# Pooled attention and expert routing on one core: batches in pairs, pooling by accumulated transposes, x scattered straight into expert slots

## The chip, the cores and the metric

One core of a Trainium2 chip. The metric is the device time of one execution in microseconds (us); where several executions are given, the median. The kernel before takes 391.01 us (two runs, 390.69 and 391.33).

A ratio is the mean time of one kernel's fast runs over the mean of the other's fast runs of the same rounds, so it is not quite the ratio of the medians that are quoted. Its interval is at 95%. "Fast" leaves out runs marked slow (a lower clock, or over 1.5% above the fastest of the same kernel).

## The reference

Attention in which keys and values are averaged over groups of 8 positions (576 become 72), then a layer of experts in which each token's expert is given.

```python
B, H, S, D = 8, 8, 576, 64
k_p = k.reshape(B, H, 72, 8, D).mean(axis=3)        # and v_p
scores = (1/8) * q @ k_p.T                          # softmax over 72
x = attn(q, k_p, v_p) -> [B*S = 4608, H*D = 512]
for e in range(8):                                  # domain_id: int64[4608], 0..7
    mask = domain_id == e
    out[mask] = relu(x[mask] @ w1[e]) @ w2[e]       # w1 512x1024, w2 1024x512
```

All inputs are float32, the sums are float32 in the kernel and the operands float16. The draw is fixed: the experts have 497 to 615 tokens.

## The kernel before

Attention runs batch by batch. x is written to memory in token order, then, when the last batch is stored, each expert gathers its rows (6 blocks of 128, 704 columns used), transposes them on TensorE, and runs two layers. The parts that matter:

```python
# attention: divide by the softmax sum, plain order in x_sb
nc.vector.tensor_tensor(out=x_sb[0:rows, g, D*h0:D*(h0+4)]..., in0=xq[0:rows, :, 1:65],
                        in1=rcp[0:rows, :].to_broadcast([rows, 4, D]), op=ALU.mult)
nc.sync.dma_start(dst, x_sb[:, 0:4, :])              # x_nat, once per batch
# ... cut ...
# experts: gather, transpose on PE, two layers, scatter
for j in range(6):
    nc.gpsimd.indirect_dma_start(out=gth[:, j], in_=x_nat[:], in_offset=orig_sb[:, e, j:j+1], ...)
# ... cut ...
osem = nc.alloc_semaphore(f"osem{e}")
with tc.tile_critical(name=f"osc{e}"):
    for j in range(6):
        nc.gpsimd.indirect_dma_start(out=out, out_offset=orig_sb[0:rows, e, j:j+1], 
                                     in_=o_sb[0:rows, j, :], ...).then_inc(osem, 16)
    nc.gpsimd.wait_ge(osem, 16 * 6)                  # one wait for all six
if e + 2 < E:
    gs[e + 2] = moe_xload(e + 2, ...)
    wlds[(e + 2) % 3] = moe_wload_hw(e + 2)          # float32 by the ScalarE queue, cast on VectorE
```

The six output scatters of an expert go out one behind the other and are waited for once, at the end. The weights of experts 2 to 7 do not go through GpSimd's queue at all: they are fetched as float32 on another queue and cast on VectorE.

The softmax here doesn't subtract the row's maximum and nothing guards it: scores larger than these inputs give would overflow.

Of the kernel before, what the change touches and what calls it, by code (L numbers as in the profile page):

```python
# [9 lines left out]
BF16 = mybir.dt.bfloat16  # L10
I32 = mybir.dt.int32
U32 = mybir.dt.uint32

AFT = mybir.ActivationFunctionType
ALU = mybir.AluOpType

B = 8
H = 8
S = 576
D = 64  # L20
HD = H * D
SP = S // 8
N = B * S
FF = 1024
E = 8
CAP = 704
CAPB = 768
NSLOT = E * CAPB
NBLK = NSLOT // 128
SENT = 1 << 20  # L30
NCH = 36
# [3 lines left out]
def kernel(  # L35
# [11 lines left out]

    const = ctx.enter_context(tc.tile_pool(name="const", bufs=1))
    dram = ctx.enter_context(tc.tile_pool(name="dram", bufs=1, space=bass.MemoryType.DRAM))
    persist = ctx.enter_context(tc.tile_pool(name="persist", bufs=1))  # L50

    x_nat = dram.tile([N, HD], F16)

    iota_row = const.tile([128, 128], I32)
    nc.gpsimd.iota(iota_row[:], pattern=[[1, 128]], base=0, channel_multiplier=0)
    iota_col = const.tile([128, 1], I32)
    nc.gpsimd.iota(iota_col[:], pattern=[[0, 1]], base=0, channel_multiplier=1)
    iota_row_f = const.tile([128, 128], F32)
    nc.vector.tensor_copy(iota_row_f[:], iota_row[:])
    iota_col_f = const.tile([128, 1], F32)  # L60
    nc.vector.tensor_copy(iota_col_f[:], iota_col[:])
    ident_f = const.tile([128, 128], F32)
    nc.vector.tensor_scalar(out=ident_f[:], in0=iota_row_f[:], scalar1=iota_col_f[:, 0:1],
                            scalar2=None, op0=ALU.is_equal)
    ident_h = const.tile([128, 128], F16)
    nc.vector.tensor_copy(ident_h[:], ident_f[:])
    Ls = const.tile([128, 128], F32)
    nc.vector.tensor_scalar(out=Ls[:], in0=iota_row_f[:], scalar1=iota_col_f[:, 0:1],
                            scalar2=None, op0=ALU.is_gt)
    ones_row = const.tile([128, 128], F32)  # L70
    nc.vector.memset(ones_row[:], 1.0)
    def band_tile(name, w, off, ncols):
        bt = const.tile([128, ncols], F16, name=name)
        pw = const.tile([128, 1], F32, name=name + "_pw")
        nc.vector.tensor_scalar(out=pw[:], in0=iota_col_f[:], scalar1=1.0 / w, scalar2=float(off),
                                op0=ALU.mult, op1=ALU.add)
        pwm1 = const.tile([128, 1], F32, name=name + "_pwm1")
        nc.vector.tensor_scalar(out=pwm1[:], in0=pw[:], scalar1=-1.0, scalar2=None, op0=ALU.add)
        q1 = const.tile([128, ncols], F32, name=name + "_q1")
        nc.vector.tensor_scalar(out=q1[:], in0=iota_row_f[:, 0:ncols], scalar1=pw[:, 0:1],  # L80
                                scalar2=None, op0=ALU.is_le)
        q2 = const.tile([128, ncols], F32, name=name + "_q2")
        nc.vector.tensor_scalar(out=q2[:], in0=iota_row_f[:, 0:ncols], scalar1=pwm1[:, 0:1],
                                scalar2=None, op0=ALU.is_gt)
        nc.vector.tensor_tensor(q1[:], q1[:], q2[:], op=ALU.mult)
        nc.vector.tensor_scalar(out=bt[:], in0=q1[:], scalar1=0.125, scalar2=None, op0=ALU.mult)
        return bt
    P2 = band_tile("P2", 2, 0, 64)
    Ptail = band_tile("Ptail", 8, 0, 8)
    tokid_i = const.tile([128, NCH], I32)  # L90
    nc.gpsimd.iota(tokid_i[:], pattern=[[1, NCH]], base=1, channel_multiplier=NCH)
    tokhi_i = const.tile([128, NCH], I32)
    nc.vector.tensor_scalar(out=tokhi_i[:], in0=tokid_i[:], scalar1=6, scalar2=None,
                            op0=ALU.logical_shift_right)
    toklo_i = const.tile([128, NCH], I32)
    nc.vector.tensor_scalar(out=toklo_i[:], in0=tokid_i[:], scalar1=63, scalar2=None,
                            op0=ALU.bitwise_and)
    tokhi = const.tile([128, NCH], F32)
    nc.vector.tensor_copy(tokhi[:], tokhi_i[:])
    toklo = const.tile([128, NCH], F32)  # L100
    nc.vector.tensor_copy(toklo[:], toklo_i[:])

    orig_sb = persist.tile([128, E, 6], I32)
    posf = persist.tile([128, NCH], F32)
    blkf = persist.tile([128, NCH], F32)

    def pe_warmup(wps, n_mm, mv, k_parts=128):
        for i in range(n_mm):
            nc.tensor.matmul(wps[0:128, 0:512], ident_h[0:k_parts, :], mv,  # L109
                             start=(i == 0), stop=(i == n_mm - 1))  # L110

    with tc.tile_pool(name="rt", bufs=1) as rt, \
         tc.tile_pool(name="rtp", bufs=1, space=bass.MemoryType.PSUM) as rtp:
        dom2 = rt.tile([128, NCH, 2], I32)
        nc.sync.dma_start(dom2[:], moe_domain_id.bitcast(I32).rearrange(
            "(p c two) -> p c two", p=128, two=2))
        domf = rt.tile([128, NCH], F32)
        nc.vector.tensor_copy(domf[:], dom2[:, :, 0])
        oh = rt.tile([128, NCH, E], F32)
        for e in range(E):  # L120
            nc.vector.tensor_scalar(out=oh[:, :, e], in0=domf[:], scalar1=float(e),
                                    scalar2=None, op0=ALU.is_equal)
        rowtot = rt.tile([128, E], F32)
        nc.vector.tensor_reduce(out=rowtot[:], in_=oh[:].rearrange("p c e -> p e c"),
                                op=ALU.add, axis=mybir.AxisListType.X)
        a_ps = rtp.tile([128, E], F32, space=bass.MemoryType.PSUM)
        nc.tensor.matmul(a_ps[:], Ls[:], rowtot[:], start=True, stop=False)
        erow_i = rt.tile([128, E], I32)
        nc.gpsimd.iota(erow_i[:], pattern=[[1, E]], base=0, channel_multiplier=0)
        erow = rt.tile([128, E], F32)  # L130
        nc.vector.tensor_scalar(out=erow[:], in0=erow_i[:], scalar1=float(CAPB), scalar2=None,
                                op0=ALU.mult)
        nc.tensor.matmul(a_ps[:], ones_row[0:1, :], erow[0:1, :], start=False, stop=True)
        bpre = rt.tile([128, NCH, E], F32)
        nc.vector.memzero(bpre[:, 0, :])
        for c in range(1, NCH):
            nc.vector.tensor_tensor(bpre[:, c, :], bpre[:, c - 1, :], oh[:, c - 1, :], op=ALU.add)
        abase = rt.tile([128, E], F32)
        nc.vector.tensor_copy(abase[:], a_ps[:])
        tmp = rt.tile([128, NCH, E], F32)  # L140
        for e in range(E):
            nc.vector.tensor_scalar(out=tmp[:, :, e], in0=bpre[:, :, e], scalar1=abase[:, e:e + 1],
                                    scalar2=None, op0=ALU.add)
        nc.vector.tensor_tensor(tmp[:].rearrange("p c e -> p (c e)"),
                                tmp[:].rearrange("p c e -> p (c e)"),
                                oh[:].rearrange("p c e -> p (c e)"), op=ALU.mult)
        slotf = rt.tile([128, NCH], F32)
        nc.vector.tensor_reduce(out=slotf[:], in_=tmp[:], op=ALU.add, axis=mybir.AxisListType.X)
        slot_i = rt.tile([128, NCH], I32)
        nc.vector.tensor_copy(slot_i[:], slotf[:])  # L150
        pos_i = rt.tile([128, NCH], I32)
        nc.vector.tensor_scalar(out=pos_i[:], in0=slot_i[:], scalar1=127, scalar2=None,
                                op0=ALU.bitwise_and)
        blk_i = rt.tile([128, NCH], I32)
        nc.vector.tensor_scalar(out=blk_i[:], in0=slot_i[:], scalar1=7, scalar2=None,
                                op0=ALU.logical_shift_right)
        nc.vector.tensor_copy(posf[:], pos_i[:])
        nc.vector.tensor_copy(blkf[:], blk_i[:])
    scale = 1.0 / 8.0
    mw = ctx.enter_context(tc.tile_pool(name="mw", bufs=3))  # L160
    with tc.tile_pool(name="ld", bufs=3) as ld_pool, \
         tc.tile_pool(name="qp", bufs=2) as qp, \
         tc.tile_pool(name="vp_p", bufs=3) as vp_p, \
         tc.tile_pool(name="ap", bufs=3) as ap_pool, \
         tc.tile_pool(name="xp", bufs=2) as xp, \
         tc.tile_pool(name="rt2", bufs=2) as rt2, \
         tc.tile_pool(name="gp_ps", bufs=4, space=bass.MemoryType.PSUM) as gp_ps, \
         tc.tile_pool(name="sct_ps", bufs=1, space=bass.MemoryType.PSUM) as sct_ps, \
         tc.tile_pool(name="op_ps", bufs=1, space=bass.MemoryType.PSUM) as op_pool, \
# [53 lines left out]
        def stage_a(b):  # L223
            k_sb, v_sb, q_sb, k_tl, v_tl, q_tl = ld[b % 3]
            if b + 2 < B:
                ld[(b + 2) % 3] = attn_load(b + 2)
# [271 lines left out]
```

## Time and profile before

| stretch, us | what runs | TensorE (PE) busy |
|---|---|---|
| 0 to 17 | routing | 6 of 17 |
| 17 to 176 | attention, 8 batches of 20 us | 137 of 159 |
| 176 to 195 | hole: x stored, gathered, weights | 7 of 19 |
| 195 to 383 | 8 experts, 23.5 us each | 178 of 188 |
| 383 to 395 | last scatters | 0 |

The table is read from the busy time of each engine by stretch. Columns: stretch and its length, then busy us and instruction count of PE, PE's weight loads, VectorE (DVE), ScalarE (ACT), GpSimd (POOL), then the mean granted PE clock, the DMA share and GB/s. Kernel before:

```profile
0.00:17.00 17.00, 6.17 (x17) 2.73 (x18) 12.55 (x81) 1.72 (x4) 11.95 (x22) 1.00 1.20 142
17.00:57.00 40.00, 33.85 (x291) 20.09 (x289) 32.27 (x104) 21.87 (x36) 18.50 (x24) 0.83 1.56 198
57.00:176.00 119.00, 103.45 (x656) 54.72 (x656) 83.92 (x300) 46.18 (x81) 11.80 (x15) 0.50 0.60 104
176.00:195.00 19.00, 7.46 (x36) 3.42 (x35) 5.05 (x5) 2.15 (x4) 12.62 (x11) 0.59 0.90 336
195.00:383.00 188.00, 178.13 (x1063) 93.37 (x1062) 41.64 (x35) 83.09 (x132) 93.04 (x80) 0.97 0.48 172
```

PE is busy 178 of 188 us in the experts at clock 0.97: that stage is bound by PE, and anything that hides behind PE is free there. In attention the clock is 0.50 for most of the time.

### The profile page before, as it was taken

How to read it: one execution, taken by the hardware profiler on the slowest of the kernel's cores; microseconds unless marked ns; L12 is line 12 of the kernel's file. 1: busy time of each engine (PE TensorE's matmuls, PEld its weight loads, DVE VectorE, ACT ScalarE, POOL GpSimd, SP SyncE). 2: the span in 40 equal slices, each digit the busy share in tenths (PEclk: the TensorE clock that was granted, in tenths of full speed). 3: DMA queues.
4: the chain of work that ended last, by engine and by line, in shares of the span. 5: the costliest groups of instructions: out<-in, count | busy, mean ns of one | idle time of the engine just before them, and what ended most of it. 6: DMA issues, size and time to landing. Idle time of an engine off the chain costs nothing.

```text
span 395.3 us, 5560 instructions
## 1 busy us (share of the span) xinstructions
PE 329.1 (83%) x2060; PEld 174.3 (44%) x2060; DVE 175.4 (44%) x521; ACT 155.1 (39%) x257; POOL 153.7 (39%) x156
## 2 busy tenths in 40 slices
PE   0879879899797979852595999999999999999960
PEld 0445544527272544430252455554545454554420
DVE  6897867676957666692301233322322421001010
ACT  1147716243341616500234345362635355453410
POOL 9445425122000000007875626275266375443405
PEclk9989855555555555555669899999999999999995
DMA  8999999999601010138992729388674523211303
GB/s 108 190 190 192 192 220 196 226 210 195 132 2 60 2 61 0 61 119 313 384 336 63 265 74 337 143 276 322 221 272 129 207 64 124 104 73 52 114 1 128
DMA packets 58027, 62.80 MB, mean 159 GB/s; under 512 B 16140, under 2 KB 43278, under 8 KB 58000
## 3 DMA queue, kind: packets, MB, share of 16 engines
q0 software_dynamic: 46656, 32.53, 45.5%
q10 hardware_dynamic: 9408, 25.17, 17.8%
q1 hardware_dynamic: 1936, 4.76, 3.3%
q8 instruction: 16, 0.26, 0.3%
q14 instruction: 11, 0.09, 0.1%
HBM read 68.19 MB, written 16.25 MB: 214 GB/s over the span
## 4 chain that ended last, share of the span: by engine, by line
PE 45%; DMA 5%; issue 2%; ACT 1%; POOL 1%; DVE 1%; ACTq 0%; POOLq 0%; another core or an unknown queue 0%
PE ops L449 21%; PE hps L438 20%; DMA w_32_2696<-in_moe_w_dram 4%; PE trp L419 3%; POOL out_dram L459 1%; ACT hT L440 1%; DVE w_sb L400 1%; DMA x_nat<-x_sb 0%; ACT xsT_cur L421 0%; DVE o_sb L452 0%; ACT o_sb L454 0%; ACTq L394 0%; POOLq L493 0%; ACTq L398 0%; POOLq L459 0%
## 5 line engine op out<-in xcount | busy, mean ns | idle before, releaser
L408 POOL DMA_INDIRECT gth<-x_nat,orig_sb x48 | 57.0, 1188 | 131.0 <-DVE gth L406 87.4
L449 PE MATMUL ops<-w_sb,hT 128*128 128x512 f16 (+1 forms) x384 | 91.7, 383 | 1.0 <-ACT hT L440 0.7
L438 PE MATMUL hps<-xsT_cur,w_sb 128*128 128x192 f16 (+1 forms) x512 | 83.5, 320 | 2.8 <-ACT hT L440 1.7
L459 POOL DMA_INDIRECT out_dram<-o_sb,orig_sb x48 | 54.4, 1134 | 58.0 <-issue 25.8
L438 PEld LDWEIGHTS <-w_sb 128*128 128x128 f16 x512 | 46.9, 100 | 38.0 <-issue 8.5
L440 ACT ACTIVATE hT<-hps 128x704 f16<-128x704 f32 x64 | 48.4, 756 | 38.8 <-PE hps L438 32.4
L452 DVE COPY o_sb<-ops 128x512 f32<-128x512 f32 x24 | 16.6, 690 | 92.8 <-PE ops L449 84.7
L449 PEld LDWEIGHTS <-hT 128*128 128x128 f16 (+1 forms) x384 | 36.7, 100 | 42.3 <-issue 5.9
L262 PE MATMUL qt_p<-ident_h,q_sb 128*64 128x128 f16 x256 | 35.7, 279 | 5.0 <-ACT qT_sb L266 3.6
L454 ACT ACTIVATE o_sb<-ops 128x512 f32<-128x512 f32 (+1 forms) x24 | 14.3, 595 | 62.6 <-PE ops L449 53.1
L421 ACT ACTIVATE xsT_cur<-trp 128x512 f16<-128x512 f16 (+1 forms) x48 | 24.4, 561 | 30.3 <-DMA gth<-x_nat,orig_sb 24.3
L262 PEld LDWEIGHTS <-q_sb 128*64 128x64 f16 x256 | 24.7, 144 | 17.7 <-issue 15.9
L266 ACT ACTIVATE qT_sb<-qt_p 64x1024 f16<-64x1024 f16 x16 | 16.3, 1018 | 22.7 <-PE qt_p L262 22.7
L317 PEld LDWEIGHTS <-at_sb 72*128 72x128 f16 (+1 forms) x320 | 20.8, 130 | 8.2 <-DVE x_sb L322 3.6
L419 PE MATMUL trp<-ident_h,gth 128*128 128x128 f16 (+1 forms) x192 | 17.2, 222 | 7.6 <-ACT xsT_cur L421 5.5
L419 PEld LDWEIGHTS <-gth 128*128 128x128 f16 (+1 forms) x192 | 13.4, 101 | 17.3 <-issue 13.0
L238 PEld LDWEIGHTS <-P_80 128*64 128x64 f16 x64 | 8.2, 132 | 18.0 <-DVE kp_sb L246 11.5
L297 PEld LDWEIGHTS <-kpT_sb 64*72 64x72 f16 x64 | 9.0, 143 | 16.3 <-issue 14.1
L194 DVE TENSOR_SCALAR ohc<-iota_row_f,posf 128x128 f16<-128x128 f32 x36 | 11.0, 306 | 10.6 <-PE op_ps L204 10.6
L204 PE MATMUL op_ps<-vc,ohc 128*128 128x96 f16 x36 | 7.8, 245 | 8.5 <-DVE vc L202 8.4
L109 PE MATMUL warm_2424<-gth,ident_h 128*128 128x512 f16 x10 | 4.4, 626 | 10.7 <-DMA gth<-x_nat,orig_sb 10.7
L183 POOL DMA_DIRECT2D k_sb<-in_k_dram x8 | 7.1, 888 | 15.8 <-PE op_ps L204 11.4
(621 smaller groups left out, 431.7 us busy)
## 6 DMA issues: line engine op xcount, KB each, us to landing
q_sb<-in_q_dram POOLq DMA_DIRECT2D x8, 512.0 KB
k_sb<-in_k_dram POOLq DMA_DIRECT2D x8, 512.0 KB
v_sb<-in_v_dram POOLq DMA_DIRECT2D x8, 512.0 KB
x_nat<-x_sb SPq DMA_DIRECT2D x8, 512.0 KB, 2.6
w_sb<-in_moe_w_dram POOLq DMA_DIRECT2D x4, 1024.0 KB
w_32_2692<-in_moe_w_dram ACTq DMA_DIRECT2D x1, 2048.0 KB
w_32_2696<-in_moe_w_dram ACTq DMA_DIRECT2D x1, 2048.0 KB
w_32_2919<-in_moe_w_dram ACTq DMA_DIRECT2D x1, 2048.0 KB
```

Source lines behind the costliest of these rows:

```text
L262: nc.tensor.transpose(qt_p[:, hl, t, :], q_sb[:, 2 * hp + hl, t, :], ident_h[:])
L266: nc.scalar.activation(qT_sb[:, 2 * hp:2 * hp + 2, 0:512], qt_p[:], AFT.Copy)
L317: nc.tensor.matmul(xq[0:rows, hh, :], at_sb[0:72, h, cols], vp_sb[0:72, h, :], start=True, stop=True)
L408: nc.gpsimd.indirect_dma_start(out=gth[:, j], out_offset=None, in_=x_nat[:], in_offset=bass.IndirectOffsetOnAxis(ap=orig_sb[:, e, j:j + 1] ...
L419: nc.tensor.transpose(trp[:, kk, 0:cols], gth[0:cols, j, 128 * kk:128 * (kk + 1)], ident_h[0:cols, 0:cols])
L421: nc.scalar.activation(dst[:, :, 128 * j:128 * j + cols], trp[:, :, 0:cols], AFT.Copy)
L438: nc.tensor.matmul(hps[:, c0:c0 + cn], w1_sb[:, kk, 128 * f:128 * (f + 1)], xsT[:, kk, c0:c0 + cn], start=(kk == 0), stop=(kk == 3))
L440: nc.scalar.activation(hT[:, f, :], hps[:, 0:CAP], AFT.Relu)
L449: nc.tensor.matmul(ops[0:rows, :], hT[:, f, 128 * j:128 * j + rows], w2_sb[:, f, :], start=(f == 0), stop=(f == 7))
L452: nc.vector.tensor_copy(o_sb[0:rows, j, :], ops[0:rows, :])
L454: nc.scalar.activation(o_sb[0:rows, j, :], ops[0:rows, :], AFT.Copy)
L459: nc.gpsimd.indirect_dma_start(out=out, out_offset=bass.IndirectOffsetOnAxis(ap=orig_sb[0:rows, e, j:j + 1], axis=0), in_=o_sb[0:rows, j, ...
```

## The change

Its intent: take work off VectorE and PE, and remove the hole and the trip of x through memory in token order. Batches are handled in pairs. Keys and values are loaded in tiles whose partition is a pooling group, so that one load has runs of 18 KB, and PE pools them by transposing the 8 members of each group into the same accumulator. The slot of every token is worked out before attention starts. Each finished block of 128 tokens is scattered directly to its slots in `x_slots` and comes back by DMA transposes, so PE transposes nothing for the experts. An expert has 640 slots, not 704 and 6 blocks; a loop for overflow is there but finds no token. The first 384 slots of experts 0 and 1 may start during the last pair. The core of the diff, cut:

```diff
-            k_sb = ld_pool.tile([128, H, 4, D], F16, tag="k_sb")          # per batch, many short runs
+        t = io.tile([128, 72, D], F16, tag=tag, bufs=2, name=tag)         # per pair, 18 KB runs
+        nc.gpsimd.dma_start(t[:]..., t_ap[2*pr:2*pr+2].rearrange("b h (g t) d -> (b h g) (t d)", g=8))
-                            nc.vector.tensor_reduce(out=dst, in_=src, op=ALU.add, ...)
+                    for t in range(8):                                    # pooled transposes
+                        for half in range(2):
+                            nc.tensor.matmul(pv[64*half:64*half+64, w, :], kk[:, 8*(w0+w)+t, :], ident[:],
+                                             start=(t == 0), stop=(t == 7), skip_group_check=True)
-            nc.sync.dma_start(dst, x_sb[:, 0:4, :])
+            xo = x_sb[:].rearrange("p (b h a) -> p h a b", b=4, h=H)[:, 4 * qd:4 * qd + 4]
+            nc.vector.tensor_tensor(out=xo, in0=pv[:, :, 0:64].rearrange("p h (a b) -> p h a b", b=4), ...)
+            if qd == 1:
+                nc.gpsimd.indirect_dma_start(out=x_slots[:], out_offset=slot_i[:, c:c+1], in_=x_sb[:], ...)
-                    nc.tensor.transpose(trp[:, kk, 0:cols], gth[0:cols, j, 128*kk:128*(kk+1)], ...)
+            nc.sync.dma_start_transpose(xT[:, :, 0:s1 - s0], x_slots[CAP*e + s0:CAP*e + s1, :])
-            w1_32 = ws.tile([128, 4, FF], F32, tag="w1_32")
-            nc.scalar.dma_start(w1_32[:], ...);  nc.vector.tensor_copy(w1_sb[:], w1_32[:])
+            nc.gpsimd.dma_start(w1[:]..., moe_w1[e].rearrange("(p k) f -> p (k f)", k=4))  # all experts
-            with tc.tile_critical(name=f"osc{e}"):                        # six scatters, one wait
+                nc.gpsimd.indirect_dma_start(out=out, out_offset=orig[:, bl:bl+1], in_=y[:], ...)
```

Every GpSimd DMA goes into one software queue (q0 in the trace). Nothing in the diff says that scatters wait for each other, but each one writes `x_slots` or `out` as a whole as far as dependency tracking can see, because the rows are known only at run time. So each one is held back until the previous one has landed. The reordered write of x (`p h a b`) matches the row order of the new `w1` load.

## The prediction

> **What bounds the kernel now.** The engine table by stretch (391.0 us timed, 395.3 profiled) shows four stages. 0 to 17 us: routing. 17 to 176 us: attention, 20 us per batch; until about 100 us the DMA is full (190 to 210 GB/s written, twice that read, as loads cast f32 to f16), afterwards PE and DVE wait on each other; the granted PE clock is 0.50 from 57 to 201 us. 176 to 195 us: a hole, in which x is stored and gathered and a weight load holds the chain 16.3 us (chain of waits). 195 to 383 us: eight experts, PE busy 178 of 195 us at clock 0.96, so PE-bound, 23.5 us each. Tail of scatters: 12 us.
>
> **Removed.** (1) Experts compute 640 columns and 5 blocks instead of 704 and 6. In the trace 64 first-layer matmuls took 9.65 us and 41 second-layer ones 9.07 us, so columns run at 2.4 GHz; 640 slots cost 8.5+8.5=17.1 us per expert, against 9.4+10.2 plus 1.3 of PE transposes and bubbles. All experts: 137 us of PE against a stage of 188. The largest expert has 615 tokens, so the overflow loop should not run. (2) The hole: x goes out as it is made, and two experts' first 384 slots start inside the last pair. (3) DVE's pooling reductions (64 of 0.68 us) and weight casts (12 of 2.3 us). (4) The tail: scatters go out as blocks finish.
>
> **Added.** (1) Routing is longer and stands before attention in PE's order: some 80 DVE instructions (0.17 us small, 0.45 us at 288 elements), 109 small matmuls, four 1152-wide comparisons (estimate 1.3 us) each waiting for PE. Estimate: first pooling matmul at 45 us instead of 16. Loads run meanwhile (six of 2.36 MB, 40 us at the 370 GB/s read rate seen). (2) Pooling on PE: 196 matmuls per pair. With transposes, scores and values, 43k columns per pair: 23 us at full clock, 37 us at half. (3) Each scatter of x and of the output waits until the previous one landed. A 128-row scatter took 2.7 us to land: x costs about 22 us per pair, output 15 us per expert beside PE's 17. (4) Ten DMA transposes, of which this trace has none. The Trainium skill, "DMA: Bandwidth & Descriptors" (other measured facts), gives 261 GB/s: an estimate of 2.5 us plus latency, hidden except after pairs 2 and 3.
>
> **Sum.** Routing 45; first pooling 12; pairs 0 to 2 at 30 each; pair 3 with expert 0's early part 30, including 7 us waiting for pair 2's last scatters; other experts 126 of PE plus 10 of layer turns and 4 waiting; tail 7: about 322 us.
>
> **Clock.** The Trainium skill, "TensorE: Matmul & The Clock Gate" (Part 1), says a busy window releases the half clock and an idle one restores it; the trace agrees in kind (1.00 in most of 17 to 57 us, 0.50 in loosely fed attention, 0.96 with experts). Dense pooling bursts should keep pairs mostly fast; all slow gives about 360, all fast 305.
>
> **What would show it.** Chain: routing until 45 us, then PE. Pair period 27 to 38 us; 17 to 19 us per full expert at clock near 1; DVE busy falls from 175 to about 130 us; POOL's scatters wait on earlier DMAs; PE waits at most about 10 us for xT.
>
> **What would make it wrong.** Transposes far slower than 261 GB/s; serial scatters slowed by weight loads above 3.4 us each, which makes POOL the experts' bound; attention all at half clock; routing longer than 55 us.
>
> Predicted: 322 us, 8 in 10 within 292 to 360; faster by over 2% 0.93, within 2% 0.04, slower 0.03.

## More of the kernel before

The groups of instructions (line, engine, operation, output and input tiles, count, then busy us and mean ns of one, then idle time before the group with what ended it), and one execution of the division that writes x (least, median and most ns, then its start). Kernel before:

```profile
L449 PE MATMUL ops<-w_sb,hT 128*128 128x512 f16 (+1 forms) x384 | 91.7, 383 | 1.0 <-ACT hT L440 0.7
L459 POOL DMA_INDIRECT out_dram<-o_sb,orig_sb x48 | 54.4, 1134 | 58.0 <-issue 25.8
L438 PEld LDWEIGHTS <-w_sb 128*128 128x128 f16 x512 | 46.9, 100 | 38.0 <-issue 8.5
```

```profile
L322 DVE TENSOR_TENSOR x_sb<-b_673,rcp x1: 405/405/405, 46.3 to 46.3; 128x256 f16<-128x256 f32 x1
```

Read the second line for what it does not say: of POOL's 58 us of idle before output scatters, 25.8 us is ended by nothing in the profile ("issue") and the rest by other engines' work, none of it by an earlier DMA. The division takes 0.41 us for 256 columns.

The landing times (from issue until all bytes are written) of the output scatters, least, median and most, first in the kernel before, then in the changed kernel; the third line is that of the changed kernel's x scatters:

```profile
DMA to landing us min/median/max: 2.0/2.7/2.7
DMA to landing us min/median/max: 2.6/2.8/13.1
DMA to landing us min/median/max: 2.4/2.4/26.7
```

## The result and the profile after

Changed kernel: 443.27 us (442.43 and 444.12); before 391.01 us. Ratio 1.1363, interval 1.1241 to 1.1485. The prediction of 322 us, 292 to 360, was wrong in size and direction.

The same stretches for the changed kernel (0 to 47 routing and first pooling, then four pairs, experts, tail):

```profile
0.00:47.00 47.00, 18.33 (x318) 16.55 (x319) 26.70 (x93) 2.79 (x5) 7.16 (x17) 0.75 0.88 191
47.00:80.00 33.00, 25.05 (x380) 19.11 (x378) 27.79 (x45) 16.33 (x26) 5.99 (x6) 0.78 0.38 89
80.00:123.00 43.00, 21.04 (x316) 15.38 (x315) 22.14 (x38) 13.38 (x22) 8.36 (x11) 0.62 0.69 148
123.00:157.00 34.00, 23.06 (x340) 16.87 (x338) 26.11 (x43) 14.59 (x23) 8.98 (x11) 0.70 0.29 71
157.00:223.00 66.00, 28.38 (x204) 16.84 (x204) 28.67 (x47) 14.18 (x23) 14.57 (x16) 0.66 0.30 72
223.00:414.00 191.00, 142.23 (x773) 95.84 (x772) 40.51 (x59) 32.36 (x54) 45.13 (x51) 0.85 0.60 136
414.00:441.00 27.00, 2.06 (x10) 0.73 (x8) 0.69 (x1) 0.60 (x1) 3.92 (x4) 0.61 0.10 38
```

The boundary at 80 us is late: the second pair's first matmul starts at 75.1 us, so the first pair took 28 us and the second 48.

Compare the expert rows. PE's work fell from 178 to 142 us (some of the fall is expert 0's first 384 slots, which ran in the last pair), and the stage still takes 191 us in place of 188: PE is no longer the bound. The last pair needs 66 us for 28 us of PE work.

The groups of instructions of the changed kernel that answer to those of before:

```profile
L514 PEld LDWEIGHTS <-w 128*128 128x128 f16 x512 | 71.9, 149 | 94.1 <-issue 67.0
L442 DVE TENSOR_TENSOR x_sb<-small,rcp 128x256 f16<-128x256 f32 x72 | 93.5, 1299 | 22.9 <-DMA x_slots<-x_sb,slot_i 19.3
L530 PE MATMUL small<-w,hT 128*128 128x512 f16 x320 | 72.8, 386 | 0.3 <-DVE y L535 0.3
L539 POOL DMA_INDIRECT out_dram<-y,orig x40 | 39.8, 995 | 149.1 <-DMA out_dram<-y,orig 117.5
```

The output matmuls (L530) take 386 ns each, as before (383): PE has not become slower. POOL's idle before an output scatter is now ended by an output scatter's own landing, for 117.5 us in all. And the division that writes x takes 1299 ns where it took 405.

The waits of the changed kernel (engine, line, what it waited for: us in all, times, longest):

```profile
POOL out_dram L539 <- DMA out_dram<-y,orig: 117.5, 25, 12.8
...
POOL x_slots L447 <- DMA x_slots<-x_sb,slot_i: 47.1, 9, 26.4
...
PE big L514 <- DMA xT<-x_slots: 42.0, 2, 28.0
```

The timeline of GpSimd (start, duration, instruction, in brackets the idle before it and what ended it) shows one step of each chain. First in the second pair, then in the experts:

```profile
87.76 0.61 POOL L71 DMA_DIRECT2D q<-in_q_dram  x1
88.34 0.59 POOL L486 DMA_DIRECT2D w<-in_moe_w_dram  x1
...
91.70 1.03 POOL L447 DMA_INDIRECT x_slots<-x_sb,slot_i  x1 [1.18 <-DVE x_sb L442]
119.16 1.02 POOL L447 DMA_INDIRECT x_slots<-x_sb,slot_i  x1 [26.42 <-DMA x_slots<-x_sb,slot_i]
```

```profile
262.93 0.60 POOL L486 DMA_DIRECT2D w<-in_moe_w_dram  x1
263.51 0.59 POOL L489 DMA_DIRECT2D w<-in_moe_w_dram  x1
266.12 1.04 POOL L539 DMA_INDIRECT out_dram<-y,orig  x1 [2.03 <-DVE y L535]
279.05 1.01 POOL L539 DMA_INDIRECT out_dram<-y,orig  x1 [11.89 <-DMA out_dram<-y,orig]
```

A scatter of x normally lands in 2.4 us (median). The one issued at 91.70 stands in the same queue behind q, w1, w2, k and v issued from 87.8 on, and lands just before 118.5. Meanwhile no further x block may go out, the buffers of x fill, and PE and DVE stop from about 104 to 119. VectorE's line at the end of that stop:

```profile
118.46 1.30 DVE L442 TENSOR_TENSOR x_sb<-small,rcp 128x256 f16<-128x256 f32 x1 [16.16 <-DMA x_slots<-x_sb,slot_i]
```

In the experts the first scatter after each pair of weight loads lets the next go only 10.7 to 13.9 us later, six times; the others follow at about 3.5 us, or when their block is ready. That sets the length of an expert: its five scatters need about 12 + 4 x 3.5 = 26 us where a load stands between them, against 17.7 us of PE work (8.9 us for the first layer and 8.8 us for the second, read from the last good version below).

The largest stop is in the last pair. PE stands 28 us in the middle of its attention work, because a filled-in piece of expert 0 in its program order waits for the transposed x:

```profile
192.01 1.47 PE L514 MATMUL big<-xT,w 128*128 128x384 f16 x4 [28.00 <-DMA xT<-x_slots]
```

The scatters of the third pair went one by one, and the last landed at about 179 us; then two transposes needed another 12 us beside a weight load. The shortfall by stage, with the terms of the prediction:

| stage | predicted | measured | error |
|---|---|---|---|
| routing | 45 | 37.7 | -7 |
| first pooling | 12 | 9.2 | -3 |
| pairs 0 to 2 | 90 | 110.3 (28, 48, 34) | +20 |
| pair 3 | 30 | 66.2 | +36 |
| experts | 140 | 190.9 | +51 |
| tail | 7 | 26.5 | +19 |
| sum | 324 | 440.8 | +117 |

### The profile page after: what moved, and what is told of

It is laid out like the page before. It is cut to its first block, busy times and chain, and to the rows that moved or that the text cites. A ratio compares the mean times of both kernels' runs of the same rounds, so it can differ in the third digit from the quotient of the medians.

```text
span 440.8 us, 5605 instructions
## 1 busy us (share of the span) xinstructions
PE 260.2 (59%) x2328; PEld 181.3 (41%) x2328; DVE 172.6 (39%) x321; ACT 94.2 (21%) x153; POOL 94.1 (21%) x113
## 5 line engine op out<-in xcount | busy, mean ns | idle before, releaser
L514 PE MATMUL big<-xT,w 128*128 128x320 f16 (+2 forms) x512 | 89.4, 337 | 78.1 <-DMA xT<-x_slots 42.0
L514 PEld LDWEIGHTS <-w 128*128 128x128 f16 x512 | 71.9, 149 | 94.1 <-issue 67.0
L442 DVE TENSOR_TENSOR x_sb<-small,rcp 128x256 f16<-128x256 f32 x72 | 93.5, 1299 | 22.9 <-DMA x_slots<-x_sb,slot_i 19.3
L520 DVE TENSOR_SCALAR hT<-big 128x640 f16<-128x640 f32 (+2 forms) x40 | 28.4, 711 | 122.8 <-PE big L514 120.9
L530 PE MATMUL small<-w,hT 128*128 128x512 f16 x320 | 72.8, 386 | 0.3 <-DVE y L535 0.3
L539 POOL DMA_INDIRECT out_dram<-y,orig x40 | 39.8, 995 | 149.1 <-DMA out_dram<-y,orig 117.5
L447 POOL DMA_INDIRECT x_slots<-x_sb,slot_i x36 | 35.6, 990 | 144.2 <-DVE rcp L439 63.7
L530 PEld LDWEIGHTS <-hT 128*128 128x128 f16 x320 | 31.6, 99 | 36.8 <-issue 2.3
L416 ACT ACTIVATE at<-big 72x576 f16<-72x576 f32 x64 | 40.0, 644 | 27.9 <-PE big L413 26.8
L535 DVE COPY y<-small 128x512 f32<-128x512 f32 x20 | 14.0, 702 | 63.8 <-PE small L530 37.7
L413 PE MATMUL big<-qT,kpT 64*72 64x288 f16 x128 | 24.2, 379 | 10.2 <-DVE hT L520 4.1
## 6 DMA issues: line engine op xcount, KB each, us to landing
x_slots<-zt ACTq DMA_DIRECT2D x1, 1536.0 KB, 19.3
```

The costliest lines, as they stand in the source:

```text
L413: nc.tensor.matmul(p[0:72, par, 0:288], s["kpT"][64 * par:64 * par + 64, bh, :], s["qT"][64 * par:64 * par + 64, :, 8 * bh:8 * bh + 8], st ...
L416: nc.scalar.activation(at[0:72, bh % 8, :].rearrange("p (a c) -> p a c", a=2), p[0:72, :, 0:288], AFT.Exp, scale=1.0 / 64.0)
L442: nc.vector.tensor_tensor(out=xo, in0=pv[:, :, 0:64].rearrange("p h (a b) -> p h a b", b=4), in1=rcp[:].unsqueeze(2).unsqueeze(3).to_broad ...
L447: nc.gpsimd.indirect_dma_start(out=x_slots[:], out_offset=bass.IndirectOffsetOnAxis(ap=slot_i[:, c:c + 1], axis=0), in_=x_sb[:], in_offset ...
L514: nc.tensor.matmul(p[:, a, 0:m], w1[:, kk, fi:FF:8], xT[:, kk, m * a:m * a + m], start=(kk == 0), stop=(kk == 3))
L520: nc.vector.tensor_scalar(out=dst, in0=p[:, 0:nh, 0:m], scalar1=0.0, scalar2=None, op0=ALU.max)
```

## The experiments

Theory A: the time goes to *gates*, scatters that wait for the landing of the previous one. Theory B: it goes to the *place in the queue*, loads in front of scatters. Theory C: VectorE's slow write of x. Theory D: PE's program order in the last pair, and the overflow branch, that is, details. They are not exclusive, so each is removed alone, then together. The expectations use the letters otherwise: their A is A and B here, their B is C here, and their C says that the DMA engines are simply full.

The changed kernel took 443.27 and 443.86 us in its two groups of runs, and two variants that left its time alone took 443.59 and 445.28 us on another chip, while the kernel before varied by 3%; so differences between variants of the changed kernel are given in us too, against the control. Only the variants without overflow branch, without any gates and with the loads earlier ran on the control's chip; the other differences compare two chips. All runs but one gave the reference's result.

### Control: the changed kernel again

> The changed kernel itself, as a control on the same chip as the next three. All theories: ratio to the kernel before 1.13 to 1.14.

443.86 us, ratio 1.1048 (1.0945 to 1.1152), before 402.29 us on that chip. The expected ratio was missed, not because the changed kernel moved but because the kernel before took 11 us more on this chip.

### The write of x in plain order

```diff
-            xo = x_sb[:].rearrange("p (b h a) -> p h a b", b=4, h=H)[:, 4 * qd:4 * qd + 4]
+            xo = x_sb[:, 256 * qd:256 * qd + 256].rearrange("p (h d) -> p h d", h=4)
...
-            nc.gpsimd.dma_start(w1[:]..., moe_w1[e].rearrange("(p k) f -> p (k f)", k=4))
+            nc.gpsimd.dma_start(w1[:], moe_w1[e].rearrange("(k p) f -> p k f", k=4))
```

> Only the order in which the vector engine writes x changes (256 elements in a row instead of every 128th), and the first-layer weights are loaded in the matching row order, so the result stays right. Theory A (the software DMA queue: every scatter waits for the one before it, and each big load that is queued ahead of a scatter is added to the chain): the x write falls from 1.30 us to about 0.41 us as in the kernel before, but the scatters of a pair still cost 9 x 3.2 us = 29 us, so at most 5 us per pair is won: 420 to 435 us. Theory B (the strided write makes the vector engine the bound of the attention pairs; 72 x 0.89 = 64 us of it): pairs 0 to 2 fall from 33 to 43 us each to 25 or less, 380 to 405 us.

430.48 us, ratio 1.0704 (1.0641 to 1.0766): 13 us better than the control. The group of the division, in the kernel with the plain write:

```profile
L442 DVE TENSOR_TENSOR x_sb<-small,rcp 128x256 f16<-128x256 f32 x72 | 30.5, 424 | 38.3 <-DMA x_slots<-x_sb,slot_i 36.0
```

VectorE's time fell by 63 us (93.5 to 30.5), and only 13 us came back. The rest of the line shows where it went: VectorE now waits 36 us for x scatters, against 19 before. The stretched write costs real time, but most of it was hidden under the gates. (The order of the first weights' load had to change with it; its part was not measured.)

### No gate on the output scatters

```diff
-                nc.gpsimd.indirect_dma_start(
+                ins = nc.gpsimd.indirect_dma_start(
                     out=out, out_offset=..., in_=y[:], ...)
+                tc.declare_no_dep(ins, group="outs", reason="rows of out are disjoint")
+                tc.add_to_no_dep_group("outs", ins)
```

Every token has one row of `out`, so the scatters may overlap.

> The output scatters no longer wait for each other (their rows are disjoint); the weight loads stay in the same queue, nothing else changes. Theory A: the stage after the last pair is 191 us because each scatter waits for the one before and so for the weight load before that; without the wait the stage falls to about 150 us, total 395 to 410. Theory C (the DMA engines are simply full with weights, so that the scatters are late in any case): under 10 us won, 433 or more.

405.65 us, ratio 1.0108 (1.0028 to 1.0188): 38 us. The expert stage, from the last attention matmul to the last matmul, shrinks from 192 to 165 us and the tail with it. In this kernel no wait of GpSimd for an earlier output scatter is left in the list of waits.

### Weights off GpSimd's queue, gates kept

```diff
-        wload(2)
+        wload_hw(2)          # float32 by the SyncE queue into freed k, v, q buffers, cast on VectorE
...
-                wload(e + 3)
+            wload_hw(...)    # the same for experts 3 to 7, casts spread over the second layer
```

> Experts 2 to 7 get their weights over the hardware queue of SyncE as f32 and VectorE casts them (about 1.15 us per quarter); output scatters still wait for each other. Same bytes read, twice as many written to SBUF. Theory A: no scatter is queued behind 4 MB of weights, so the six waits of 10 to 13 us in the expert stage shrink to under 4 us each and the run takes 390 to 405 us. Theory C (bandwidth): the bytes are what counts, the scatters stay as late; 435 to 450 us.

427.59 us, ratio 1.0635 (1.0579 to 1.0691): 16 us. The scatter behind a load no longer waits for the load to be finished in its queue, but it still does not go out at 3.5 us. GpSimd's timeline in this kernel:

```profile
249.25 0.97 POOL L565 DMA_INDIRECT out_dram<-y,orig  x1 [3.44 <-DVE y L561]
256.57 1.38 POOL L565 DMA_INDIRECT out_dram<-y,orig  x1 [6.34 <-DMA out_dram<-y,orig]
264.64 1.56 POOL L565 DMA_INDIRECT out_dram<-y,orig  x1 [6.69 <-DMA out_dram<-y,orig]
```

A dozen steps of 6 to 9 us stand in place of six of 10.7 to 13.9: B is a part of the cost, as far as this run shows not the larger one. The rest is the gate with a slower landing. The Trainium skill, "DMA: Bandwidth & Descriptors", Issuing engines are not separate DMA queues, says that DMAs of all issuing engines run on the same 16 DMA engines and interleave; steps that stay twice as long as 3.5 us agree with it. VectorE also waited 42 us for staged loads and did the casts, so this run does not price B cleanly.

### No weight loads in the experts (wrong result)

```diff
-                wload(e + 3)
+                wt[e + 3] = wt[e]
```

> Wrong on purpose: experts 3 to 7 reuse the weights of experts 0 to 2, so five loads of 4.2 MB in the expert stage are not issued; the output scatters still wait for each other. e3 won only 16 us by moving these loads to another queue. If the cost is the scatters' chain being held up by the loads at all, by place in the queue or by sharing the engines: no scatter takes over 4 us, the stage is bound by about 3.5 us x 5 scatters = 17.5 us per expert, close to PE's 17.1, and the run is 45 to 55 us under the control (390 to 400). If the chain itself is the cost, with or without loads: at most 20 us under it.

403.0 us, ratio 1.032 (1.0238 to 1.0402), about 40 us below the changed kernel's time. The output has a relative error of 1.09, as it must. That lies between the two forecasts. Without loads for experts 3 to 7 most scatters there follow at 3.5 us, and the expert stage (as measured for the free output scatters) falls from 192 to 152 us: the whole gain is there. So in this stage the cost is the gates and the loads together: taking out the gates alone left 165 us, taking out these loads alone 152. The kernel is still slower than before because the loads in front of the x scatters, expert 2's load and the late transposes remain: attention ends at 225.0 us, where the kernel before starts its experts at 195.

### The loads earlier, gates kept

```diff
+        wload(0)                       # after the first six loads
...
+                qt_[pr + 2] = load_pair(q, pr + 2, "q")   # beside k and v
+            if pr == 2:
+                wload(1)
```

> Only the place of loads: q of pair p+2 is issued with its k and v before the pair's scatters instead of behind them, the weights of expert 0 behind the first six loads, those of expert 1 at the start of pair 2; the waits between scatters stay. Theory A (place in the queue): the 27 us in which the scatter at 92 us lies behind 11 MB goes, and PE's stop of 16 us with it, and the transposes before pair 3 run without a weight load beside them (12 us for two becomes 5 to 7): 20 to 30 us under the control. Theory C (the bytes are what counts): within 8 us of the control.

434.54 us, ratio 1.0823 (1.074 to 1.0905): 9 us, where 20 to 30 were expected. Moving the loads away from the scatters in program order is worth much less than removing what makes their order matter.

### The filled-in expert at the end of the last pair

```diff
-            run(merge(scav_units(pr), fill, 0.4 if pr + 1 < NP else 0.0))
+            run(merge(scav_units(pr), fill, 0.4 if pr + 1 < NP else 1.0))
```

> One constant: the early part of expert 0 is put after the last pair's units instead of between them. Theory A: PE's 28 us wait for xT at the start of pair 3 (the scatters of pair 2, in a chain, then the transposes beside a weight load) goes, and its 10 us of early work come later: 15 to 25 us won, 418 to 428 us. If that wait only hid the scatters' chain, which then stalls PE after pair 3 instead: within 8 us of 443.

434.5 us, ratio 1.0847 (1.0753 to 1.0941): 9 us. That is between the two forecasts, near the second. The 28 us stop of PE in the last pair was real, and PE's wait for transposes is gone (42.0 to 0.7 us); but the time went to waits for gated scatters that it had covered. VectorE's wait for x buffers grew from 19.3 to 33.9 us, ScalarE's for output buffers from 28.5 to 50.4. Waits of this kernel:

```profile
DVE x_sb L442 <- DMA x_slots<-x_sb,slot_i: 33.9, 3, 16.5
PE big L514 <- DMA xT<-x_slots: 0.7, 1, 0.7
ACT y L537 <- DMA out_dram<-y,orig: 50.4, 5, 12.4
```

### No overflow branch

The block after `nblk = nc.values_load(...)` is removed; no token of this input uses it.

> The overflow loop that never runs with this data is taken out, with its load of the count and its branches. In the trace of the changed kernel nothing is recorded in the last 14 us after the last scatter's issue, of which the scatter itself needs 3 to 4. If the branches around the loop cost the rest: 8 to 11 us less than the control. If it is only the end of the last scatters: within 2 us of it.

437.81 us, ratio 1.0895 (1.0808 to 1.0981): 6 us, a little under the 8 to 11 expected. Theory D is worth 6 plus 9 us.

### No gates at all

```diff
+                tc.declare_no_dep(ins, group="xs", reason="rows of x_slots are disjoint")
+                tc.add_to_no_dep_group("xs", ins);  xscat.append(ins)
...
+            for p_ in xscat:           # a transpose waits for every x scatter issued before it
+                tc.add_manual_dep(ins, p_.name, ...)
```

together with the free output scatters.

> As e2_free_out, and the x scatters don't wait for each other either (each transposing load waits for all of them). Theory A in the form 'the chain of waits alone': the x scatters of pair 2 are down before pair 3 starts, PE's wait for xT there falls from 28 us to about 10, and the run falls 15 to 25 us under e2, to a ratio of 0.94 to 0.98. Theory A in the form 'the place in the queue': the scatters of pair 1 still stand behind 11 MB of loads issued just before them, so PE's 16 us stop in pair 1 stays, and at most 15 us are won over e2: ratio 0.97 to 1.01.

380.06 us, ratio 0.945 (0.9358 to 0.9543): 64 us better than the control, and now faster than before. GpSimd's timeline of this kernel in the second pair, to be read against the step from 91.70 to 119.16 above:

```profile
91.36 1.03 POOL L448 DMA_INDIRECT x_slots<-x_sb,slot_i  x1 [8.97 <-DVE x_sb L443]
93.39 1.01 POOL L448 DMA_INDIRECT x_slots<-x_sb,slot_i  x1 [1.00 <-DVE rcp L440]
94.75 0.98 POOL L448 DMA_INDIRECT x_slots<-x_sb,slot_i  x1 [0.35 <-DVE x_sb L443]
97.27 0.98 POOL L448 DMA_INDIRECT x_slots<-x_sb,slot_i  x1 [1.53 <-DVE rcp L440]
114.43 0.98 POOL L448 DMA_INDIRECT x_slots<-x_sb,slot_i  x1 [16.18 <-DVE rcp L440]
```

Scatters go out as blocks finish. A stop from 97 to 114 remains: the blocks themselves are late there, and VectorE still waits once, 8.9 us, for a scatter that holds an x buffer behind the loads. Those 8.9 us are B without gates.

### No gates and the plain write

> e6 (no scatter waits for another) plus the plain order of x. Theory B, now that the chain no longer covers it: pairs 0 to 2 are bound by the vector engine in e6 (28 us without stops), so they fall to 23 us or less, and the run falls by 15 to 30 us from e6's 380. If PE or the loads bind the pairs: under 8 us.

348.6 us median of two fast runs (344.95, 343.72) and two slow ones (353.69, 352.24); before 389.59 us. The means of the fast ones give 344.3 / 389.6 = 0.884. The same edit that was worth 13 us under the gates is worth 24 us of the kernel before's time by ratio (0.945 less 0.884, of 395 us) and 36 us by plain difference, on another chip. Either way about twice as much or more: VectorE's extra time had been hidden, not absent.

### Tuned: early loads, no gates, plain write

```diff
+                wload(2)               # at the start of the last pair; loads as in the early-loads run
-            run(merge(scav_units(pr), fill, 0.4 if pr + 1 < NP else 0.0))
+            run(merge(scav_units(pr), fill, 0.4))
-                y = late.tile([128, HD], F32, tag="y", bufs=4, name="y")
+                y = late.tile([128, HD], F32, tag="y", bufs=5, name="y")
```

> e7 plus the early loads of e8, expert 2's weights before pair 3's scatters, expert 0's early part 40% into pair 3 and five y buffers. The stops left in e6 (9 us in pair 1, 12 us for xT in pair 3, 10 us and more at the start of the expert stage) go in part: 15 to 35 us under e7. If these stops only move: within 8 us of e7.

335.33 us (fast runs 329.31 and 333.77, slow ones 336.89 and 340.27), ratio 0.8495 (0.8386 to 0.8604). The profile shows one large stop left, in the experts. The second line is the same stop in the profile of the next kernel:

```profile
239.24 10.55 PE L522 MATMUL big<-xT,w 128*128 128x320 f16 x64 [32.34 <-DMA xT<-x_slots]
238.40 10.95 PE L518 MATMUL big<-xT,w 128*128 128x320 f16 x64 [23.14 <-DMA xT<-x_slots]
```

The transpose for that expert was issued at 186.1 us, with weight loads issued at 184, 191 and 209 us, and landed at 239.1; its packets moved from 190.2 to 234.5 us. In this profile transposes take 3.3, 9.0 and 53.0 us from issue to landing (least, median, most).

### Tuned, with part of the routing moved into the pairs

The table of output rows is built during pairs 0 and 1, not before attention.

> e10 with the building of the output order (14 us of VectorE and PE before attention) moved into pairs 0 and 1, where it is not on the path. If routing before attention costs what the chain shows, the first pooling matmul comes at 19 to 24 us instead of 37.7 and the run is 10 to 16 us under e10; if the loads bind the first pair instead: at most 5.

343.39 us (fast runs 336.9 and 341.81), ratio 0.8814 (0.8732 to 0.8896). A miss: the first pair starts at 28.7 us in place of 47, but the first three pairs take 44, 36 and 25 us where they took 24, 29 and 24. The expectation's reason, that the loads bind the first pair, is not what the trace shows: PE waits for no load there. Its largest stop is 10.6 us, behind VectorE, which waits 10.9 us for an x scatter to land that was issued behind the third pair's k, v and q; twice in each of the first two pairs PE also waits 3 to 4 us for the table's own VectorE work. The rest was not taken apart.

### All transposes ahead of the weight loads

```diff
-        xload(*xnext.pop(0))
+        xnext[1:3] = [xnext[2], xnext[1]]
+        for t in xnext:
+            xload(*t)                  # all remaining transposes, into freed k, v, q buffers
         for t in tasks:
-            if xnext:
-                xload(*xnext.pop(0))
             run(expert_units(*t))
```

> As e10, but all remaining transposes of x are issued together right after the last attention pair, into the freed key, value and query buffers, ahead of the weight loads of experts 3 to 7. Theory (a transposed load of 256 B packets starves when weight loads with 8 KB packets are queued beside it): TensorE's wait for transposed x falls from 43 us (e10) to 12 us at most and the time from 335 us to 305 to 315 us. Rival (the transposes wait for the last scatters of x, or the lost time of e10 moves to the weights): within 8 us of e10, 327 to 343 us, with the wait moved to weights or left at the first transpose.

Fast runs 310.08 and 311.47 us, slow ones 320.91 and 345.15; before 397.81 us; the means of the fast runs give 310.8 / 397.7 = 0.781. PE's wait for transposed x falls from 42.9 to 6.3 us. The stretch from 180 to 300 us, first in the tuned kernel, then with the transposes ahead:

```profile
180.00:300.00 120.00, 87.58 (x526) 63.86 (x525) 25.22 (x35) 21.95 (x35) 30.92 (x34) 0.87 1.05 166
```

```profile
180.00:300.00 120.00, 119.82 (x724) 86.50 (x723) 34.95 (x49) 29.92 (x49) 41.01 (x45) 1.00 0.86 187
```

PE is busy 119.82 of 120 us at full clock: the expert stage is PE-bound at last, as the prediction had it. The loads are the same and most are issued behind the transposes now. The stop of 32 us came from a transpose that was issued late and then starved beside weight loads: 44 us for packets that take 3 us alone. Even here the last two transposes are slow (issued at 192.3 and 216.8 us, done at about 236 and 245), but PE does not need them yet. The edit also gives the transposes more buffers; order and buffers were not tried apart.

### The same with the second weights in natural row order

```diff
-            nc.gpsimd.dma_start(w2[:]..., moe_w2[e].rearrange("(p k) f -> p (k f)", k=8))
+            nc.gpsimd.dma_start(w2[:], moe_w2[e].rearrange("(k p) f -> p k f", k=8))
-                        nc.tensor.matmul(p[:, a, 0:m], w1[:, kk, fi:FF:8], ...)
+                        nc.tensor.matmul(p[:, a, 0:m], w1[:, kk, 128 * fi:128 * fi + 128], ...)
```

> e15 with the second weight matrix in natural row order, so that the stationary operands of the first layer are contiguous columns, and the loads have 2 KB runs in place of 16 KB ones. If the strided stationary columns cost TensorE time (149 against 100 ns for one weight load in the records), the expert stage shrinks by up to 2048 x 0.05 us = 10 us at most, if they are hidden behind matmuls less than 3 us. If long runs matter to the loads, the loads land later and the time grows by over 5 us.

312.87 us (312.18 to 313.65, four runs), ratio 0.7865 (0.7834 to 0.7895). One weight load on PE fell from 149 to 98 ns, and the time did not move: 2 us above the fast runs of the version before it, so it hides behind matmuls. (The expectation's product is wrong: 512 such loads at 0.05 us each are 26 us, not 10.) Long runs in the second weights' load are not what made the change fast or slow either. It is the steadiest of the fast versions here, and it beats both kernels.

```profile
L525 PEld LDWEIGHTS <-w 128*128 128x128 f16 x512 | 50.1, 98 | 33.9 <-issue 13.7
```

### The last two edits with the gates in place

The changed kernel with only the transposes issued together:

> The changed kernel with only the transposes of x issued together before the expert stage, all gates of the scatters left. Theory (the gates on the output scatters bound the expert stage, transposes do not): within 2% of the changed kernel (435 to 450 us where the kernel before takes 391 to 402), although the waits for transposed x fall. Rival (starved transposes cost the expert stage much by themselves): 15 to 40 us faster.

445.28 us, ratio 1.1202 (1.1162 to 1.1241): nothing. PE's wait for transposed x stays at 41.9 us, so the expectation that it would fall was wrong. The gated scatters of the last pair run until 232 us, the transposes go out at 236 us, and weight loads are already queued at 233: with gates the transposes cannot be got ahead of the loads.

The changed kernel with only the natural row order of the second weights:

> The changed kernel with only the second weight matrix in natural row order: short runs, contiguous stationary columns. Theory (the scatter behind each weight load waits for the bytes, not for the run length): within 1.5% of the changed kernel (437 to 450 us); the scatter interval behind each weight load stays at 10 to 14 us. Rival (long packets hold the engines and starve the scatters): the interval behind each load falls below 7 us and the time falls by 10 us or more.

443.59 us, ratio 1.1172 (1.1121 to 1.1222): nothing, and the scatters behind the loads still take 12 to 14.5 us. The length of the runs is not what holds them; what is in front of them is.

## Why the prediction was wrong

- **"Each scatter of x and of the output waits until the previous one landed. A 128-row scatter took 2.7 us to land: x costs about 22 us per pair, output 15 us per expert beside PE's 17."** This is the step that failed. The mechanism was right and seen in advance; its size was not. With nothing in front a step takes 3.5 us (output) and 3.2 us (x), not 2.7, so a pair's nine x scatters need 29 us and not 22. Worse, a scatter that stands behind loads let the next one go only after 10.7 to 13.9 us (output), and an x scatter took 26.7 us to land. Five output scatters then need 26 us, so they no longer hide beside PE's 17.7, as the sum had them do. Taking the gates out alone gave 64 us. The text itself named this as what would make it wrong ("serial scatters slowed by weight loads above 3.4 us each"), then priced it at 4 us of waiting.
- **"pair 3 ... 30, including 7 us waiting for pair 2's last scatters."** Measured 66 us, with a stop of 28 us. The gated scatters of pair 2 ended only at 179 us, 22 us after the pair; then came the transposes, 12 us.
- **"Ten DMA transposes ... 2.5 us plus latency, hidden except after pairs 2 and 3."** With no weight load beside it, the packets of a transpose of 655 KB took about 3.1 us (3.05 to 3.22, three of them in the trace): near enough. From issue to landing the ten took 5.0 to 17.4 us, 8.2 in the median, and up to 53 us in the tuned kernel. Once the gates were gone, getting the transposes ahead of the loads was worth 21 us between the fast runs of two chips, and 27 us by ratio (0.8495 less 0.781, of 395 us).
- **"DVE busy falls from 175 to about 130 us."** It was 172.6. The division that writes x was taken at its old 0.41 us; the diff shows the new output order, with neighbouring elements 256 bytes apart, and it took 1.30 us, 72 times. The Trainium skill would have warned: "Vector Engine (DVE) Microarchitecture Reference", 5.2, lists 1.71 to 2.51 ns per column for a destination that steps at every element, against 1.05 contiguous. By that page, an estimate of 256 x 2.51 + 75 ns = 0.72 us. With the plain order VectorE's total was 118.7 us.
- **"tail 7."** 26.5 us. The last scatter is issued 425.9 us into a span of 440.8; the chained steps before it make up most of the rest, and the overflow branch 6 us. Part of the last 15 us carries no recorded work and stays open.
- **Right:** routing (45 predicted, 37.7 measured) and the first pooling (12, 9.2), both on the safe side; the PE work of the experts (17.7 us each in the last good version, 142 for eight, against 137; at the changed kernel's lower clock the two layers took 89.4 and 72.8 us). In part right: that dense work lifts the clock. The Trainium skill, "TensorE: Matmul & The Clock Gate", Part 1, was cited for it, and the clock is 1.00 once nothing interrupts PE (180 to 300 us with the transposes ahead), 0.85 in the gated experts. But the pairs ran at 0.62 to 0.78, not "mostly fast", and in the kernel before PE counts as busy for 103 of 119 us of attention at clock 0.50: the busy share alone does not tell the clock.

So the expected gain existed. It was covered first by the gates, then by VectorE's stepped write, then by starved transposes. With those three removed and some loads moved earlier, the design runs in 311 to 313 us, near the 322 that was predicted for it as written. The terms are near too: routing, first pooling, pairs 0 to 2, pair 3, experts and tail take 37, 9, 84, 37, 134 and 10 us in the last good version, where 45, 12, 90, 30, 140 and 7 were predicted. This does not save the prediction: it was made for a kernel with the gates. Not settled: how far a scatter behind a load would be sped up by a separate queue alone, since that run also paid casts; and why four versions without gates (plain write, both tuned ones, transposes ahead) had two slow runs of four each, and the last good one none.

## What to carry to other kernels

When DMAs write to rows chosen at run time, find out before anything else whether each will wait for the landing of the previous one, and then price one step by the worst thing that can stand in front of it in its queue, not by its median. A cost that is hidden under a larger one looks small or zero in a single-edit experiment: the same two edits (plain write, transposes first) gave 13 and 0 us under the gates, and at least 24 and 21 us without them. Small transfers that PE waits for (turned x) belong ahead of large loads that it does not yet need, and the way to see it is the landing time least, median and most, not the median alone.

## What the Trainium skill lacked or had wrong

- "DMA: Bandwidth & Descriptors", Anatomy of one DMA, gives a software-queue DMA 2.0 us + bytes / 436e3: by that page, an estimate of 2.60 us for an output scatter of 262,144 bytes. That agrees with the fastest landing (2.6 us, median 2.8). The fit has no term for what stands in front in the queue: landings up to 13.1 us behind two weight loads, 26.7 us behind five loads.
- The same page, Latency and other measured facts, gives transposes 261 GB/s, and its Rules for kernel authors say that "A transpose next to ordinary DMAs needs nothing". For safety no run here contradicts it; for time it does. 655 KB took 3.1 us with no weight load beside it (655,360 bytes / 3.1 us = 211 GB/s), and up to 53 us from issue to landing beside weight loads. Its Queues, rings and completion order section says that an engine takes turns between queue rows a packet at a time; that fits, but no run here shows the turns themselves.
- The same page gives no time per step for a chain of row scatters that wait for each other's completion: 3.2 to 3.5 us per step here, for a landing of 2.4 to 2.8 us.
- "Vector Engine (DVE) Microarchitecture Reference", 5.2, measures stepping destinations with 4-byte words only (up to 2.51 ns per column). With 2-byte elements 256 bytes apart the runs show 1299 ns for 256 columns, against 424 ns for the same operation written in order.
- "TensorE: Matmul & The Clock Gate", Weight-path perf modes, allows column steps up to 1,024 in the fast weight load and names no cost. A weight load of 128 columns with step 8 took 149 ns in the changed kernel, and 98 ns with columns side by side in the last good version; hidden behind matmuls, it cost no time.
